# Tail subtraction and state addition moved onto TensorE in the first attention chunks

## The chip, the cores and the metric

The kernel runs on one core of a Trainium2 chip. The metric is device time in microseconds, the median of several executions. The engines are named as the profile names them: PE (TensorE matmuls), PEld (TensorE weight loads), DVE (VectorE), ACT (ScalarE), POOL (GpSimd), and SP, whose queue issues most DMAs.

## The reference, cut to what matters

A linear attention with a decaying state feeds a dense squared-ReLU layer (`_moe_ref`), and that feeds a top-2 mixture of eight experts. Only the attention's recurrence and the first product of the dense layer bear on the change:

```python
for t in range(S):                                    # S = 768, B = 4, H = 8, D = 48
    cur = einsum('bhd,bhe->bhde', u * k[t], v[t])
    y[t] = einsum('bhd,bhde->bhe', r[t], state + cur)
    state = w * state + einsum('bhd,bhe->bhde', k[t], v[t])
x = y as (B*S, H*D)                                   # 3072 x 384
h = x @ w_in;  g = max(h, 0)**2;  x2 = g @ w_out      # then the experts on x2
```

## The kernel before

**Chunks.** The 768 steps of a batch are cut into six chunks of 128, 24 chunks `q` in all; `c = q % 6` is the chunk's place in its batch. A chunk is worked through by steps: `pre` (r*k*u on POOL, and `pre_k`, the scaled keys `kp`), `p_tr` (r and k transposed on PE, copied out as `rT` by DVE and `kT` by ACT), `pre2` (the diagonal: `dg` on DVE, then `am` = ident times `dg` by eight ACT instructions, and `vx`, a small copy of parts of v), `p_a` (the scores r·k on PE into two PSUM banks, laid over `am` by DVE's `copy_predicated`, L468), `p_y` in two parts (y from the state `Z`, then from `am` and v, into one bank), `p_kv` (keys times values on PE, then the new state), and `p_x` (y split for the dense layer).

**State.** In `p_kv`, for `c > 0`, DVE adds the old state to the key-value product (L515, two instructions, one for each half of the partitions), and POOL multiplies the sum by the decay `wmid` (L516, two instructions). For `c == 0` DVE multiplies alone (L518). The last chunk of a batch makes no state.

**Split.** The dense layer's products are made of reduced-precision parts: `p_x` writes `x1h`, the rounded y (ACT, L527), and `x1l`, what rounding left (DVE, L528, y minus `x1h`). `mm1` (L545) multiplies both with the weights' parts; in its very first call the three `x1l` products come last.

**Weights.** While the first chunks run, the 16 pieces of `w_in` and `w_out` are turned from float64 into parts: `conv_w1` on ACT (L273), `conv_w2` on DVE (L280 to L292, four instructions on 128x768 elements), `conv_w3` on ACT (L302) and POOL (L303). A piece lands in one of two buffers `stg`; the end of `conv_w2` frees it and starts the DMA of the next but one.

**Order.** Engines run their instructions in the order of writing. `HEAD` (L27) lists the steps of chunks 0 to 3, with `warm n` = n idle transposes on PE and `load` for DMAs; the tables `CHUNKS` and `CONV_AT` place the steps of later chunks and weights between the dense layer's 16 pairs of `mm1` and `mm2` (L576, L570). PSUM banks of the name `att` are three in rotation, `ph` two: a step that takes a bank waits for the reader of what stood there three (two) banks ago.

Of the kernel before, what the change touches and what calls it, by code (L numbers as in the profile page):

```python
# [8 lines left out]
F32 = mybir.dt.float32  # L9
F32R = mybir.dt.float32r  # L10
BF = mybir.dt.bfloat16
I32 = mybir.dt.int32
AF = mybir.ActivationFunctionType
OP = mybir.AluOpType
# [3 lines left out]
P = 128  # L18
# [5 lines left out]
OWN_ACT = 8  # L24
KP_POOL = (2, 3, 4, 5, 6, 7, 8)

HEAD = ("load_w 0", "p_tr 0 r", "p_tr 0 k", "tables a", "spread", "pre 0",  # L27
# [8 lines left out]

CHUNKS = (((0.72, 2.09, 0.63, 0.83, 1.23, 3.2, 1.96, 5.12, 6.53),
# [56 lines left out]
def body(ctx, tc, r, k, v, w, u, w_in, w_out, w_gate, w_noise, noise, w1, w2, out):  # L94
    nc = tc.nc
    B, H, S, D = r.shape
# [10 lines left out]
    BLK = 512  # L107
    TPB = BLK // P
# [16 lines left out]
    def pool(name, side="left", stack=ctx, **kw):  # L125
        return stack.enter_context(tc.tile_pool(name=name, bufs=1, side=side, reuse_waits="tile", **kw))
# [33 lines left out]
    ident = consts.tile([P, P], F32, name="ident")  # L160
# [11 lines left out]
    def bank(tag="att", bufs=3):  # L172
        return ps.tile([P, 512], F32, name=tag, tag=tag, bufs=bufs)
# [3 lines left out]
    m1 = pool("m1", stack=c_ctx)  # L177
# [30 lines left out]
    def load_next(q):  # L208
        if q < QD or q >= NCH:
            return  # L210
        if q == QD:
            for nm, t in zip("rk", rpt):
                nc.gpsimd.memset(t, 0.0)
                turned[nm] = t.rearrange("p (a x) -> p a x", a=HP)
        load(q, "r")
        b, c = divmod(q, CPB)
        for nm in "rk":
            src = SRC[nm][b, :, c * P:(c + 1) * P, :].rearrange("(a j) s d -> j a (s d)", j=2)
            for j in range(2):
                for o in range(0, D, 32):  # L220
                    nc.sync.dma_start(turned[nm][64 * j + o:64 * j + o + 32, :, :TQ * D - o],
                                      src[j].rearrange("a (s x) -> s a x", x=TQ * D)[:, :, o:])
# [98 lines left out]
    pb = bank()  # L321
# [38 lines left out]
    def warm(n):  # L360
        pw = xops.tile([P, KD, BLK], F32, name="xo")
        for _ in range(n):
            nc.tensor.transpose(pw[:, 0, :P], ident, ident)

    Z = [at.tile([P, HP, 2 * D], F32, name=f"Z{i}") for i in range(2)]
    for t in Z:
        nc.gpsimd.memset(t, 0.0)
# [19 lines left out]
    x1h, x1l = {}, {}  # L387
# [16 lines left out]
    def pairs(q):  # L404
        return L[q]["v"].rearrange("p (a s) d -> p a (s d)", s=2)

    def ends(q):
        t = vx[q % 2].rearrange("p a s x -> p (a s x)")
        return bass.AP(tensor=t.tensor, offset=t.offset, ap=[t.ap[0], [64, HP], [48, 2], [1, 16]])
# [4 lines left out]
    def pre2(q):  # L414
        a, l = A[q], L[q]
        t = a["rk"]
        dg = at.tile([P, H], F32, name="dg", bufs=2)
        nc.vector.tensor_reduce(dg, t, axis=AX.X, op=OP.add)

        own = nc.scalar.copy if q <= TPB else nc.gpsimd.tensor_copy  # L420
        own(ends(q), pairs(q)[:, :, 32:64].rearrange("p a (s x) -> p a s x", s=2))
        a["am"] = at.tile([P, H, P], F32, name="am", tag="am", bufs=2)
        if q < OWN_ACT:
            for h in range(H):
                nc.scalar.activation(a["am"][:, h, :], ident, AF.Copy, scale=dg[:, h:h + 1])
        else:
            nc.gpsimd.tensor_mul(a["am"], ident[:, None, :].to_broadcast([P, H, P]),
                                 dg[:, :, None].to_broadcast([P, H, P]))


    def p_tr(q, which, *tag):
# [41 lines left out]
    def p_y(q, part):  # L473
# [6 lines left out]
        def add(g, x, y, **kw):  # L480
            d, n = divmod(g, 4)
            nc.tensor.matmul(pb[32 * n:32 * n + 32, d, :], x, y, skip_group_check=True, **kw)  # L482

        if part == 0:
            for g in range(KD * 4 if c else 0):
                hp, s = divmod(g, 3)
                add(g, Z[c % 2][:KR, hp, 32 * s:32 * s + 32], a["rT"][:KR, hp, :], start=(g < 4), stop=False)
            return
# [10 lines left out]
    def p_kv(q, *tag):  # L499
        c = q % CPB  # L500
        if c == CPB - 1:
            return
        pb = bank(*tag)[:, :HP * D].rearrange("p (a d) -> p a d", d=D)
        kf = kp[q % 2].rearrange("p h x -> p (h x)")
        v = L[q]["v"]
        for hp in range(HP):
            for g in range(4):
                nc.tensor.matmul(pb[32 * g:32 * g + 32, hp, :], kf[:, hp * P + 32 * g:hp * P + 32 * g + 32],  # L508
                                 v[:, 2 * hp + g // 2, :], start=(hp == 0), stop=(hp == HP - 1), skip_group_check=True)
        for s in range(2):  # L510
            rows = slice(64 * s, 64 * s + D)
            zn = Z[(c + 1) % 2][rows, :, s * D:(s + 1) * D]
            w_ = wmid[rows, :, None].to_broadcast([D, HP, D])
            if c:
                nc.vector.tensor_add(zn, pb[rows], Z[c % 2][rows, :, s * D:(s + 1) * D])  # L515
                nc.gpsimd.tensor_mul(zn, zn, w_)  # L516
            else:
                nc.vector.tensor_mul(zn, pb[rows], w_)  # L518

    def p_x(q, *tag):  # L520
        j, i = divmod(q, TPB)
        if i == 0:
            x1h[j] = m1.tile([P, KD, BLK], F32R, name="x1h", bufs=2)
            x1l[j] = m1.tile([P, KD, BLK], F32R, name="x1l", bufs=2)
        src = A[q]["y"][:, :DM].rearrange("p (d t) -> p d t", t=P)
        hi = x1h[j][:, :, i * P:(i + 1) * P]
        nc.scalar.activation(hi, src, AF.Copy)  # L527
        nc.vector.tensor_tensor(x1l[j][:, :, i * P:(i + 1) * P], src, hi.bitcast(F32), op=OP.subtract)  # L528
        if q + 1 == QD:
            load_next(QD)  # L530
        del A[q], L[q]


    G, PH, XO = {}, {}, {}
    X2 = {}

    def mm1(j, f):
        ph = PH[j, f] = bank("ph", 2)
        qi, fo = divmod(f, NF // NP)
        sl = slice(fo * P, (fo + 1) * P)  # L540
        terms = [(d, wt, xt) for d in range(KD) for wt, xt in ((wih, x1h), (wih, x1l), (wil, x1h))]
        if j == f == 0:
            terms.sort(key=lambda t: t[2] is x1l)
        for n, (d, wt, xt) in enumerate(terms):
            nc.tensor.matmul(ph, wt[qi][:, d, sl], xt[j][:, d, :], start=(n == 0), stop=(n == 3 * KD - 1))  # L545

    def gsplit(j, f):
# [507 lines left out]
    def run(pieces, n):  # L1055
        for p in pieces[:n]:
            p()
        del pieces[:n]

    AW = 3  # L1060
    steps = dict(spread=spread, warm=warm, p_tr=p_tr, pre=pre, tables=tables, pre_k=pre_k, load_w=load_w, p_a=p_a, pre2=pre2, p_kv=p_kv,
                 conv_w1=conv_w1, conv_w2=conv_w2, conv_w3=conv_w3, p_y=p_y, p_x=p_x, load=load)
    for step in HEAD:
        name, *args = step.split()
        tag = ("ph", 2) if name in ("p_kv", "p_x") or "ph" in args else ()
        steps[name](*(int(x) if x.isdigit() else x for x in args if x != "ph"), *tag)

    for j in range(NB):
# [6 lines left out]
        if j + 1 < NB:  # L1075
            for i, at_ in enumerate(CHUNKS[min(j, 2)]):
                q = (j + 1) * TPB + i
                todo = [(pre, ()), (p_tr, "r"), (p_tr, "k"), (pre2, ()), (p_kv, ()), (p_a, ()), (p_y, (0,)), (p_y, (1,)),
                        (p_x, ())]
                for n, (fn, args) in zip(at_, todo):  # L1080
                    if q > TPB or fn not in (pre, p_tr):
                        put(n, fn, q, *args)
# [33 lines left out]
        for f in range(NF):  # L1116
            mm1(j, f)
            gsplit(j, f)
            for p in slots[2 * f]:
                p()  # L1120
            g = j * NF + f - LAG
            if g >= 0:
                mm2(*divmod(g, NF))
                if f == LAG - 1:
                    finish(j - 1)
            for p in slots[2 * f + 1]:
                p()
# [144 lines left out]
```

## Time and profile before

| | us |
|---|---|
| median of 3 runs | 952.46 |
| lowest, highest | 951.77, 954.32 |
| the profiled execution | 953.81 |
| its span in the trace | 952.0 |
| PE busy in the span | 938.3 |
| DVE, ACT, POOL busy | 533.7, 434.4, 345.8 |

The granted TensorE clock is 0.998 of its upper level, 2.4 GHz, over the profiled execution. The span of the trace lies 1.8 us inside the profiled execution's own time; that execution is 1.35 us above the median. In the trace an instruction has a start and a length; a length of a PE row is modelled and overlaps the next, so the pace is read from one start to the next. Waits in brackets give the idle time before a row and what ended it.

### The profile page before, as it was taken

Reading aid. Unit: us, or ns where it says so; the run is one execution under the profiler, and the core shown is the slowest. Engines: PE = TensorE matmul, PEld = TensorE weight load, DVE = VectorE, ACT = ScalarE, POOL = GpSimd, SP = SyncE. Lnnn points to the kernel's source line nnn. Section 1 sums busy time; section 2 is a strip of 40 time slices with the busy share of each in tenths; the row PEclk is TensorE's granted clock in tenths of the full one; section 3 lists DMA queues with packets and bytes.
Section 4 is the critical chain, followed back from the end, with each engine's and each line's share of the span. In section 5 each row is a group of like instructions: output and inputs, shape, how many; then the busy total and the mean of one; then the engine's idle time right before and its main releaser. Section 6 shows DMA issues by size and latency. Waiting matters only on the chain.

```text
span 952.0 us, 17757 instructions
## 1 busy us (share of the span) xinstructions
PE 938.3 (99%) x6845; PEld 805.0 (85%) x6845; DVE 533.7 (56%) x985; ACT 434.4 (46%) x798; POOL 345.8 (36%) x401
## 2 busy tenths in 40 slices
PE   9899999999999999999999999999999999999997
PEld 7677787778778778877888899999999898989987
DVE  8999757535835663583254564554545555456420
ACT  6766655334434434353555542443444444444321
POOL 6665353544563372545030353122121221212112
PEclk9999999999999999999999999999999999999999
DMA  8655379932444272342024357466645565645212
GB/s 182 161 163 164 99 192 301 245 108 64 118 121 106 55 189 57 106 108 77 1 101 98 103 137 183 108 135 135 130 97 114 121 117 109 117 94 111 33 21 37
DMA packets 193233, 112.32 MB, mean 118 GB/s; under 512 B 131777, under 2 KB 185698, under 8 KB 193122
## 3 DMA queue, kind: packets, MB, share of 16 engines
q1 hardware_dynamic: 181698, 91.03, 37.5%
q0 software_dynamic: 10624, 19.74, 11.2%
q8 instruction: 75, 1.23, 0.5%
q14 instruction: 36, 0.29, 0.1%
q10 hardware_dynamic: 800, 0.02, 0.0%
HBM read 74.64 MB, written 36.12 MB: 116 GB/s over the span
## 4 chain that ended last, share of the span: by engine, by line
PE 90%; DVE 5%; DMA 1%; issue 1%; ACT 1%; POOL 0%; POOLq 0%; ACTq 0%; DVEq 0%; SPq 0%
PE ph L545 20%; PE xo L576 19%; PE ph L866 19%; PE y L923 14%; PE y L954 4%; PE att L482 3%; PE ph L954 2%; PE att L464 2%; PE att L609 2%; PE y L866 2%; PE xo L570 1%; PE att L967 1%; DVE t L281 1%; PE att L508 1%; DVE am L468 1%
## 5 line engine op out<-in xcount | busy, mean ns | idle before, releaser
L934 POOL DMA_INDIRECT out<-yt,id x56 | 87.2, 1556 | 297.8 <-ACT yt L932 257.2
L560 DVE TENSOR_TENSOR gl<-g,gh 128x512 fp32r<-128x512 f32 x90 | 76.2, 846 | 134.9 <-ACT gh L558 131.4
L909 DVE SCALAR_TENSOR_TENSOR hl<-ph,hh 128x512 fp32r<-128x512 f32 (+1 forms) x112 | 66.9, 599 | 113.4 <-ACT hh L908 109.4
L550 ACT ACTIVATE rt<-ph 128x512 f32<-128x512 f32 x96 | 57.2, 596 | 157.9 <-PE ph L545 138.9
L545 PE MATMUL ph<-x1h,wih 128*128 128x512 f32 x288 | 119.3, 414 | 0.0
L866 PE MATMUL ph<-xh,w0h 128*128 128x512 f32 (+3 forms) x336 | 118.1, 352 | 0.0
L866 PE MATMUL ph<-xl,w0h 128*128 128x512 f32 (+3 forms) x336 | 116.2, 346 | 0.2 <-DVE xl L835 0.2
L866 PE MATMUL ph<-xh,w0l 128*128 128x512 f32 (+3 forms) x336 | 116.2, 346 | 0.0
L545 PE MATMUL ph<-x1h,wil 128*128 128x512 f32 x288 | 112.5, 391 | 0.0
L545 PE MATMUL ph<-x1l,wih 128*128 128x512 f32 x288 | 112.3, 391 | 0.0
L576 PE MATMUL xo<-gh,wol 128*128 128x512 f32 x270 | 106.2, 394 | 0.0
L908 ACT ACTIVATE hh<-ph 128x512 fp32r<-128x512 f32 (+1 forms) x112 | 58.7, 525 | 89.0 <-PE ph L866 82.1
L923 PE MATMUL y<-w1h,hh 128*128 128x384 f32 x256 | 85.7, 335 | 0.0
L923 PE MATMUL y<-w1l,hh 128*128 128x384 f32 x256 | 85.6, 334 | 0.0
L923 PE MATMUL y<-w1h,hl 128*128 128x384 f32 x256 | 85.6, 334 | 0.0
L737 POOL DMA_INDIRECT sent<-row,si x48 | 50.6, 1055 | 63.9 <-DVE gl L560 45.0
L576 PE MATMUL xo<-gh,woh 128*128 128x512 f32 x180 | 71.6, 398 | 0.0
L576 PE MATMUL xo<-gl,woh 128*128 128x512 f32 x180 | 70.2, 390 | 0.0
L866 PEld LDWEIGHTS ph<-xl,w0h 128*128 128x128 f32 x336 | 63.3, 189 | 7.7 <-DVE xl L835 0.9
L866 PEld LDWEIGHTS ph<-xh,w0l 128*128 128x128 f32 x336 | 63.2, 188 | 7.7
L866 PEld LDWEIGHTS ph<-xh,w0h 128*128 128x128 f32 x336 | 63.3, 188 | 7.0 <-ACT xh L834 0.3
L545 PEld LDWEIGHTS ph<-x1h,wih 128*128 128x128 f32 x288 | 54.0, 188 | 16.5 <-issue 3.3
(235 smaller groups left out, 2138.7 us busy)
## 6 DMA issues: line engine op xcount, KB each, us to landing
ws<-in_moe_w SPq DMA_DIRECT2D x128, 96.0 KB
ws<-in_moe_w SPq DMA_DIRECT2D x32, 384.0 KB
sent<-zero SPq DMA_DIRECT2D x8, 1375.5 KB
G<-sent SPq DMA_DIRECT2D x36, 192.0 KB
stg<-in_moe_w_in SPq DMA_DIRECT2D x8, 768.0 KB
stg<-in_moe_w_out SPq DMA_DIRECT2D x8, 768.0 KB
out<-zero SPq DMA_DIRECT2D x5, 960.0 KB
lv<-in_v SPq DMA_DIRECT2D x24, 192.0 KB
```

What stands on the lines that cost most here:

```text
L482: nc.tensor.matmul(pb[32 * n:32 * n + 32, d, :], x, y, skip_group_check=True, **kw)
L545: nc.tensor.matmul(ph, wt[qi][:, d, sl], xt[j][:, d, :], start=(n == 0), stop=(n == 3 * KD - 1))
L550: nc.scalar.activation(rt, ph, AF.Relu)
L560: nc.vector.tensor_tensor(gl, g, gh.bitcast(F32), op=OP.subtract)
L576: nc.tensor.matmul(XO[j][:, d, :], wt[qi][:, fo, sl], gt, start=(f == 0 and n == 0), stop=(f == NF - 1 and n == 2))
L737: st = nc.gpsimd.indirect_dma_start(out=sent, in_=s["row"][:, i, :], in_offset=None, out_offset=bass.IndirectOffsetOnAxis(ap=s["si"][:, i, ...
L866: nc.tensor.matmul(ph[:, c], wt[:, d, sl], xt[:, d, c], start=(m == 0), stop=(m == 3 * KD - 1))
L908: nc.scalar.activation(hh[:, :n], ph, AF.Relu)
L909: nc.vector.scalar_tensor_tensor(hl[:, :n], ph, 0.0, hh[:, :n].bitcast(F32), op0=OP.max, op1=OP.subtract)
L923: nc.tensor.matmul(py, ht[:, sl], wt[:, fo, :], start=(m == 0), stop=(m == 3 * NF2 - 1))
L934: st = nc.gpsimd.indirect_dma_start(out=out, in_=yt, in_offset=None, compute_op=OP.add, out_offset=bass.IndirectOffsetOnAxis(ap=IDX[e, un] ...
L954: nc.tensor.matmul(py[d][:, c], wt[:, fo, sl], ht[:, c], start=(m == 0), stop=(m == 3 * NF2 - 1))
```

## The change

In chunks 1 to 4 (`q <= TPB`, the second to the fifth of batch 0) PE adds the old state to the key-value product in PSUM, with two multiplications by the identity (48 rows and 192 columns each, float32, on the two halves of the partitions, into one bank); DVE then multiplies by the decay out of PSUM, and POOL's two instructions are gone. For chunks 0 to 3 the new step `p_rest` makes `x1l`: PE adds `x1h` times minus the identity (128x384) onto y's bank, and ACT copies out what remains. `p_rest 0` to `p_rest 2` stand in `HEAD`, `p_rest 3` inside the first `mm1`, behind its third product. `minus` is made by one ACT instruction ahead. In `HEAD` the ACT part of `pre2 2` now stands behind `p_rest 0`, and in all chunks `vx` is written behind `am` instead of ahead of it.

```diff
@@ pre2
-        own = nc.scalar.copy if q <= TPB else nc.gpsimd.tensor_copy
-        own(ends(q), pairs(q)[:, :, 32:64].rearrange("p a (s x) -> p a s x", s=2))
         a["am"] = at.tile([P, H, P], F32, name="am", tag="am", bufs=2)
...
+        own = nc.scalar.copy if q <= TPB else nc.gpsimd.tensor_copy
+        own(ends(q), pairs(q)[:, :, 32:64].rearrange("p a (s x) -> p a s x", s=2))
@@ p_kv
-            if c:
+            if c and q <= TPB:
+                nc.tensor.matmul(pb[rows], ident[rows, rows], Z[c % 2][rows, :, s * D:(s + 1) * D],
+                                 start=False, stop=True, skip_group_check=True)
+                nc.vector.tensor_mul(zn, pb[rows], w_)
+            elif c:
                 nc.vector.tensor_add(zn, pb[rows], Z[c % 2][rows, :, s * D:(s + 1) * D])
                 nc.gpsimd.tensor_mul(zn, zn, w_)
@@ p_x
-        nc.vector.tensor_tensor(x1l[j][:, :, i * P:(i + 1) * P], src, hi.bitcast(F32), op=OP.subtract)
+        lo = x1l[j][:, :, i * P:(i + 1) * P]
+        if q < TPB:
+            REST[q] = src, hi, lo
+        else:
+            nc.vector.tensor_tensor(lo, src, hi.bitcast(F32), op=OP.subtract)
@@ new
+    minus = m1.tile([P, BLK], F32R, name="minus", tag="rt", bufs=1)[:, :P]
+    nc.scalar.activation(minus, ident, AF.Copy, scale=-1.0)
+    def p_rest(q):
+        src, hi, lo = REST.pop(q)
+        nc.tensor.matmul(src, minus, hi, start=False, stop=True, skip_group_check=True)
+        nc.scalar.activation(lo, src, AF.Copy)
@@ mm1
+            if j == f == 0 and n == 3:
+                p_rest(TPB - 1)
@@ HEAD
-        "p_tr 2 k ph", "pre 3", "pre2 2", "warm 10", "p_a 1"
+        "p_tr 2 k ph", "pre 3", "warm 10", "p_rest 0", "pre2 2", "p_a 1"
...
-        "p_tr 3 k ph", "pre2 3", "p_a 2"
+        "p_tr 3 k ph", "p_rest 1", "pre2 3", "p_a 2"
...
-        "p_y 3 0", "p_kv 3"
+        "p_y 3 0", "p_rest 2", "p_kv 3"
```

PE between the transposes of chunk 2 and the state part of y of chunk 1 (`rp`, `kp` feed the transposes, `lv,kp` the key-value product of chunk 1, `rT,kT` its scores), before:

```order
L444 MATMUL att<-ident,rp_95 112x128 x4
L508 MATMUL ph<-lv,kp_98 32x48 x16
L444 MATMUL ph<-ident,kp_97 112x128 x4
L363 MATMUL xo<-ident 128x128 x10
L464 MATMUL att<-rT,kT 128x128 x8
L482 MATMUL att<-rT,Z_206 32x128 x12
```

And now:

```order
L448 MATMUL att<-ident,rp_95 112x128 x4
L512 MATMUL ph<-lv,kp_98 32x48 x16
L519 MATMUL ph<-Z_208,ident 48x192 x2
L448 MATMUL ph<-ident,kp_97 112x128 x4
L364 MATMUL xo<-ident 128x128 x10
L548 MATMUL att<-x1h,minus 128x384
L468 MATMUL att<-rT,kT 128x128 x8
L486 MATMUL att<-rT,Z_208 32x128 x12
```

The state's pair (L519) stands ahead of the transposes of k, and the subtraction (L548) ahead of the scores; the same two stand in the same places of chunk 2.

DVE from the scores of chunk 2 to the split of chunk 3, before:

```order
L468 COPY_PREDICATED am<-mask,att 128x4x128 x2
L280 TENSOR_SCALAR t_524<-t_524 128x768
L281 TENSOR_SCALAR t_524<-t_524 128x768
L282 SCALAR_TENSOR_TENSOR t_524<-stg,t_524 128x768
L468 COPY_PREDICATED am<-mask,ph 128x4x128 x2
L528 TENSOR_TENSOR x1l<-att,x1h 128x3x128
L292 SCALAR_TENSOR_TENSOR t_524<-stg,t_524 128x768
L449 TENSOR_TENSOR rT<-att,pow 112x512
L515 TENSOR_TENSOR Z_205<-ph,Z_206 48x4x48 x2
L528 TENSOR_TENSOR x1l<-att,x1h 128x3x128
```

And now:

```order
L472 COPY_PREDICATED am<-mask,att 128x4x128 x2
L281 TENSOR_SCALAR t_526<-t_526 128x768
L282 TENSOR_SCALAR t_526<-t_526 128x768
L283 SCALAR_TENSOR_TENSOR t_526<-stg,t_526 128x768
L472 COPY_PREDICATED am<-mask,ph 128x4x128 x2
L293 SCALAR_TENSOR_TENSOR t_526<-stg,t_526 128x768
L453 TENSOR_TENSOR rT<-att,pow 112x512
L521 TENSOR_TENSOR Z_207<-ph,wmid 48x4x48 x2
```

Two `x1l` are gone from this piece (two more stood ahead of it), and the state's add has become a multiplication of the same size.

ACT from y of chunk 2 to the dense layer's first ReLU (`rt`), before:

```order
L527 ACTIVATE x1h<-att 128x3x128
L273 ACTIVATE t_624<-stg 128x768
L527 ACTIVATE x1h<-att 128x3x128
L302 ACTIVATE wih_125<-t_524 128x768
L453 ACTIVATE kT<-att 112x512
L550 ACTIVATE rt<-ph 128x512
```

And now:

```order
L535 ACTIVATE x1h<-att 128x3x128
L274 ACTIVATE t_627<-stg 128x768
L549 ACTIVATE x1l<-att 128x3x128
L535 ACTIVATE x1h<-att 128x3x128
L303 ACTIVATE wih_125<-t_526 128x768
L457 ACTIVATE kT<-att 112x512
L549 ACTIVATE x1l<-att 128x3x128
L569 ACTIVATE rt<-ph 128x512
```

The last `x1l` of the block stands behind a weight piece and a transposed k on ACT, where DVE had made it.

## Rows read from the trace of the kernel before

**Rows 1.** Busy time by stretch: stretch, length, PE, PEld, DVE, ACT, POOL, granted clock, DMA.

```profile
12.00:42.00 30.00, 27.14 (x495) 21.50 (x495) 29.06 (x43) 20.97 (x54) 19.97 (x20) 1.00 0.75 184
42.00:73.00 31.00, 30.22 (x207) 21.68 (x207) 28.90 (x32) 20.76 (x39) 18.64 (x13) 1.00 0.54 160
73.00:400.00 327.00, 325.97 (x2602) 257.90 (x2602) 198.60 (x378) 154.30 (x274) 155.99 (x166) 1.00 0.51 138
```

**Rows 2.** The chain that ended last, in order of time: start, length, what.

```profile
23.74 0.56 DVE x1l L528
...
40.15 0.26 DVE Z L515
...
56.34 4.80 DMA stg<-in_moe_w_in
...
62.13 4.28 DMA stg<-in_moe_w_out
...
71.85 1.07 PE att L482 x28
```

**Rows 3.** Waits of PE from 8 to 80 us: total, times, longest.

```profile
PE att L482 <- DVE am L468: 0.8, 3, 0.4
```

**Rows 4.** PE in order of time: start, length, line, out<-in [idle before <-releaser].

```profile
6.95 0.91 PE L356 MATMUL att<-us 1*128 1x384 f32 x2
7.79 0.66 PE L351 MATMUL att<-ident,back 128*128 128x128 f32 x4
...
17.77 1.74 PE L464 MATMUL att<-rT,kT 48*128 48x128 f32 x16
19.59 0.86 PE L482 MATMUL att<-rT,Z 112*32 112x128 f32 x24
...
23.33 1.16 PE L464 MATMUL att<-rT,kT 48*128 48x128 f32 x16
24.43 1.20 PE L363 MATMUL xo<-ident 128*128 128x128 f32 x9
...
30.65 0.55 PE L508 MATMUL ph<-lv,kp 128*32 128x48 f32 x32 [0.89 <-DVE am L468]
...
38.71 0.49 PE L464 MATMUL att<-rT,kT 48*128 48x128 f32 x2
40.95 1.13 PE L464 MATMUL att<-rT,kT 48*128 48x128 f32 x14 [1.75 <-DVE Z L515]
```

**Rows 5.** PE near the end: products of 128x384, one behind the other.

```profile
942.32 0.33 PE L923 MATMUL y<-w1l,hh 128*128 128x384 f32 x1
942.50 0.33 PE L923 MATMUL y<-w1h,hh 128*128 128x384 f32 x1
```

**Rows 6.** DVE in order of time: state, a weight piece beside POOL, one without.

```profile
24.67 1.35 DVE L468 COPY_PREDICATED am<-mask,att 128x512 f32<-128x512 uint16 x2
...
33.81 0.56 DVE L528 TENSOR_TENSOR x1l<-att,x1h 128x384 fp32r<-128x384 f32 x1
34.28 0.68 DVE L280 TENSOR_SCALAR t<-t 128x768 f32<-128x768 f32 x1
...
40.83 1.46 DVE L280 TENSOR_SCALAR t<-t 128x768 f32<-128x768 f32 x1
...
53.14 0.55 DVE L280 TENSOR_SCALAR t<-t 128x768 f32<-128x768 f32 x1
```

**Rows 7.** ACT in order of time, around the split of chunks 0 to 3.

```profile
22.56 0.49 ACT L527 ACTIVATE x1h<-att 128x384 fp32r<-128x384 f32 x1
...
32.78 0.84 ACT L302 ACTIVATE wih<-t 128x768 fp32r<-128x768 f32 x1
33.52 0.59 ACT L453 ACTIVATE kT<-att 112x512 f32<-112x512 f32 x1
```

**Rows 8.** POOL's last state multiplication before 45 us, and who waited for L516.

```profile
41.83 1.61 POOL L516 TENSOR_TENSOR Z<-Z,wmid 48x192 f32<-48x192 f32 x2
...
  PEld att L464: 0.2, 1
```

More of the change, by code (lines that the diff above doesn't have):

```diff
@@ L25 @@
 KP_POOL = (2, 3, 4, 5, 6, 7, 8)
-HEAD = ("load_w 0", "p_tr 0 r", "p_tr 0 k", "tables a", "spread", "pre 0",
[8 rows of a table removed]
+HEAD = ("load_w 0", "p_tr 0 r", "p_tr 0 k", "tables a", "spread", "pre 0", "tables b",
[9 rows of a table added]
 CHUNKS = (((0.72, 2.09, 0.63, 0.83, 1.23, 3.2, 1.96, 5.12, 6.53),
@@ L363, in warm @@
             nc.tensor.transpose(pw[:, 0, :P], ident, ident)
+    REST = {}
+    minus = m1.tile([P, BLK], F32R, name="minus", tag="rt", bufs=1)[:, :P]
+    nc.scalar.activation(minus, ident, AF.Copy, scale=-1.0)
     Z = [at.tile([P, HP, 2 * D], F32, name=f"Z{i}") for i in range(2)]
@@ L1060, in body @@
     AW = 3
-    steps = dict(spread=spread, warm=warm, p_tr=p_tr, pre=pre, tables=tables, pre_k=pre_k, load_w=load_w, p_a=p_a, pre2=pre2, p_kv=p_kv,
+    steps = dict(p_rest=p_rest, spread=spread, warm=warm, p_tr=p_tr, pre=pre, tables=tables, pre_k=pre_k, load_w=load_w, p_a=p_a, pre2=pre2, p_kv=p_kv,
                  conv_w1=conv_w1, conv_w2=conv_w2, conv_w3=conv_w3, p_y=p_y, p_x=p_x, load=load)
```

17 rows, old and new, of the table HEAD are left out of this document.

## The prediction

> **What bounds the kernel now.** I read three views. First the busy times by stretch: from 73 us to 400 us PE is busy 325.97 of 327 us [rows 1], so whatever reaches 73 us earlier keeps its gain for hundreds of us; nothing that I see later in the trace takes it back. Between 12 and 42 us PE is busy 27.14 of 30 us, but DVE 29.06 [rows 1]: here the two hand the work to and fro, and the change lies in this stretch. Then the chain of waits: from 23.74 us on it runs through DVE (x1l at 23.74, the state's add at 40.15), then twice through a DMA of weights that a finished conversion sets off (4.80 and 4.28 us), and it passes to PE for good only at 71.85 [rows 2]. Last PE itself in order of time, for the places where it stands. It waits 0.89 us for a bank ahead of the key-value product of chunk 3 and 1.75 us ahead of the scores of chunk 4, the latter for the state's add on DVE [rows 4]; in the second part of y it waits 0.8 us in three pieces [rows 3]. One loss is no wait in the list: the scores of chunk 1 take 1.82 us (17.77 to 19.59) where those of chunk 2 take 1.10 (23.33 to 24.43) [rows 4], 0.72 lost. Together 0.9 + 1.8 + 0.8 + 0.7 = 4.2 us: no more than that can be won here, and PE gets new work that has to come out of it.
>
> **The change part by part.**
>
> *The subtraction on PE.* Four products of 128x384. Such products follow each other at 942.32 and 942.50 [rows 5], so 0.18 us each, 0.7 us in all.
>
> *The state on PE.* Four pairs of 192 columns in float32 on 48 rows, one on each half of the partitions. No such pair is in the trace. From below: the scores also run as pairs on the two halves, 8 products of 128 columns in 1.10 us [rows 4], 0.275 a pair, times 192/128 = 0.41 us. From above: one float32 product of 384 columns, so the same columns one behind the other, fills 0.84 us up to the next start (6.95 to 7.79) [rows 4]. That it costs nothing is excluded: PE has no gap at its place. I take 0.41, since the scores have the same 48 rows and halves, and keep 0.84.
>
> Here a page speaks against the change. In the scores the two halves write two banks, in the new pair one. The Trainium skill, TensorEngine Tiling (Array Packing), section Gotcha 1: PSUM Pressure, says that different row tiles cannot access the same PSUM bank simultaneously. By it the pair would run one after the other, near the upper end; by the row of the scores, near the lower. No row of this trace has two halves in one bank.
>
> *What DVE loses.* Four x1l. One takes the stretch from 33.81 to 34.28 [rows 6], 0.47 us, 1.9 us in all. The state's multiplication out of PSUM replaces an add of the same size: no difference.
>
> *What POOL loses.* Four state multiplications; the one at 41.83 took 1.61 us [rows 8]. PE was held up by this line for 0.2 us in the whole kernel [rows 8], so their going gains nothing directly. But DVE's weight instruction L280 took 1.46 us at 40.83, just ahead of that row, and 0.55 at 53.14 [rows 6]: some of DVE's instructions are longer when POOL works. With the state gone, POOL leaves DVE alone there earlier. I put 0.3 us on it, between 0 and the 0.9 that these two rows differ by.
>
> *What ACT gets.* Four x1l copies and one for `minus`. A split of the same size takes 0.49 us (22.56) [rows 7], 2.0 us in all; ACT is busy 20.97 of 30 us [rows 1]. `minus` is made ahead of the first y and has no one waiting. What stands behind the copies: the diagonal `am` of chunk 2, `am` of chunk 3, and at the end the first ReLU. `vx` behind `am` costs nothing: both are needed by the same step on PE, and `am` has to pass through DVE first. POOL's `vx` of later chunks likewise; its cover is that PE waits for nothing after 73 us [rows 1]; without it, it would cost the length of one `am`.
>
> *Walk through the block.* (1) Chunk 1: the pair and `p_rest 0` add 0.41 + 0.18 = 0.59 ahead of the scores of chunk 1. These lost 0.72 waiting for `rT`; so the end of the scores stays where it was, about 19.6. The cover is just used up. (2) Chunk 2: the pair and `p_rest 1` add 0.59 ahead of the scores at 23.33 [rows 4], with no wait there to pay for it: they start at 23.9 and end at 25.0. DVE's `copy_predicated` that reads them started at 24.67 [rows 6]; now it can't before 25.1. DVE is 0.45 us late, although it has shed two x1l: it waits for PE in their place. This is where half of the saving goes. (3) From there DVE is the bound up to 40 us, as the chain has it. It sheds the x1l of chunk 2 (0.47): even with before. PE's wait ahead of the key-value product of chunk 3 (30.65) stays, shifted by 0.4. (4) It sheds the x1l of chunk 3 (0.47): the state's add of chunk 4, at 40.15 [rows 2], is due 0.5 us earlier. (5) PE has by then got all of its new work: two more pairs and two more subtractions, 1.2 us, of which about 1.0 is visible, so it reaches the scores of chunk 4 at 38.71 + 1.0 = 39.7 and waits there until 40.95 - 0.5 = 40.45 [rows 4]: a wait of 0.75 instead of 1.75, end 0.5 us earlier. (6) On the way to 71.85 the chain is DVE, then the two DMAs, ACT, DVE [rows 2]. All of it starts with the end of a conversion, so it moves as a whole by 0.5 and by the 0.3 that POOL leaves. PE follows, because its waits of 0.8 [rows 3] are for this chain.
>
> Sum: -0.5 - 0.3 = **-0.8 us**. Against the profiled execution this is 952.0 - 0.8 = 951.2 in the span; that execution lies 1.35 us above the median, so the median should be 952.46 - 0.8 = **951.7**.
>
> **The rivals.**
>
> *A. As forecast*, 951.7, by itself 951.0 to 952.4.
>
> *B. The pair runs one after the other* (0.84), and the change is even. Each pair costs 0.43 more. Two of them stand ahead of the scores of chunk 2, so step (2) is 0.86 later, and DVE's 0.5 in step (4) turns into -0.4; PE reaches chunk 4 about when before it went on. The 0.3 of POOL is left: 952.46 + 0.4 - 0.3 = 952.5. The change then doesn't do what it is there for: DVE's free time is spent waiting for PE. For it: no gap on PE between 19.59 and 24.43 that would hide the pair, and the one bank. The page named above would give this time.
>
> *C. DVE keeps all that it sheds.* 1.9 us and the whole 0.9 of POOL would be 952.46 - 2.8 = 949.7; but steps (1) and (2) hang on scores that PE can't bring before 19.6 and 24.5 even if its new work were free, so that of the first two x1l at most 0.2 counts: 0.2 + 0.94 + 0.6 = 1.7, so 950.7, with 949.8 as the end. It needs pairs well under 0.41.
>
> *D. ACT is late with the last x1l, and the kernel is slower.* The x1l of chunk 3 now stands behind a weight piece (0.84 at 32.78, which itself waits for DVE's conversion) and `kT` (0.59 at 33.52) [rows 7], and the first dense product waits for it; the ReLU, and with it DVE's work up to the state of chunk 4, stands behind. I find x1l ready at about 35.2 and PE there at 35.1, so almost even. Each us of lateness delays PE by a us; the wait of 0.75 in step (5) and the 0.8 gained have to be used up first. It decides against the change from about 1.6 us of lateness; at 2.5 us it is +0.9, 953.4. Against it: ACT has 9 idle us in this stretch [rows 1].
>
> **How the numbers follow.** Chances: A 0.45, B 0.25, C 0.18, D 0.12. About 0.3% (2.9 us) is what a measurement of this kernel can tell from no change: faster means under 949.6, slower over 955.3. A and B lie inside by far. Of C some 0.06 lies under 949.6 (the ceiling of 4.2 allows it), of D some 0.05 over 955.3, and another 0.02 and 0.01 I give to what I have not seen. So faster 0.08, same 0.86, slower 0.06. The range goes from the end of C to D: 949.8 to 953.6, with about 0.08 left out below and 0.1 above.
>
> **What would show it.** In the profile after: the pair's length from one start to the next (0.41 or 0.84) and the subtraction's (0.18); the scores of chunk 1 ending at 19.6 again; DVE's `copy_predicated` for chunk 2 at about 25.1 with an idle time ahead of it that ends with PE; PE's wait ahead of the scores of chunk 4 cut to about 0.75 us, and their rest starting at 40.4; the first weights piece's DMA that stood at 56.34 at 55.5; the chain passing to PE at about 71.0. If DVE is not idle ahead of 25.1, step (2) is wrong. If the three x1l products in the first dense product start over 0.5 us after the sixth, D is at work. If all of this holds and the time still differs by over 1 us, something after 73 us has moved that I hold to be fixed.

## The result, and the profile after

The changed kernel takes 961.59 us (median of 4 runs, 961.49 to 962.41); the kernel before, on the same chip, 952.96 us (4 runs, 951.77 to 954.32). The ratio is 1.009, with 1.0078 to 1.0102 as its 95% interval: 8.6 us slower, where 951.7 us was forecast and 953.6 us was the end of the range. The span grew from 952.0 to 959.9 us.

Busy time by stretch after the change, with the columns of [rows 1]:

```profile
12.00:42.00 30.00, 25.34 (x454) 19.46 (x451) 22.16 (x34) 17.93 (x49) 12.62 (x11) 0.94 0.65 153
42.00:73.00 31.00, 28.49 (x212) 20.37 (x212) 24.32 (x31) 20.14 (x39) 12.46 (x8) 0.94 0.46 136
73.00:400.00 327.00, 327.00 (x2650) 258.15 (x2649) 208.95 (x379) 156.66 (x280) 162.42 (x169) 1.00 0.52 141
```

Beside [rows 1], all engines are busy for less time in the first two stretches, PE by 1.8 and 1.7 us, DVE by 6.9 and 4.6 us. No engine has become the bound; they wait for each other. And the granted clock, 1.00 before, is 0.94 in both. From 73 us on PE has no gap left, where it had 1.03 us before. So the loss lies ahead of 73 us, as the change does.

Whom PE waits for, in the whole span (total, times, longest), the lines with the change's product:

```profile
PE ph L519 <- DVE Z L521: 4.3, 3, 2.6
PE att L519 <- DVE Z L521: 2.5, 1, 2.5
```

L519 is the new product that adds the state, L521 is DVE's multiplication by the decay that stands behind it in the code. PE waits 6.8 us for the instruction that is meant to wait for PE. None of the waits of [rows 3] and [rows 4] is left in the list.

PE in order of time after the change (start, length, line, tiles, count, and the idle time ahead with what ended it):

```profile
16.77 0.52 PE L519 MATMUL ph<-Z,ident 48*48 48x192 f32 x2
19.86 0.52 PE L519 MATMUL ph<-Z,ident 48*48 48x192 f32 x2 [2.57 <-DVE Z L521]
20.31 0.65 PE L448 MATMUL ph<-ident,kp 128*112 128x128 f32 x4
20.80 1.82 PE L364 MATMUL xo<-ident 128*128 128x128 f32 x10
22.26 0.67 PE L548 MATMUL att<-x1h,minus 128*128 128x384 f32 x1
22.86 2.05 PE L468 MATMUL att<-rT,kT 48*128 48x128 f32 x16
24.84 0.86 PE L486 MATMUL att<-rT,Z 112*32 112x128 f32 x24
...
28.96 0.52 PE L519 MATMUL ph<-Z,ident 48*48 48x192 f32 x2 [0.44 <-DVE Z L521]
...
39.35 0.52 PE L519 MATMUL ph<-Z,ident 48*48 48x192 f32 x2 [1.32 <-DVE Z L521]
...
47.62 0.52 PE L519 MATMUL att<-Z,ident 48*48 48x192 f32 x2 [2.51 <-DVE Z L521]
...
81.06 0.86 PE L486 MATMUL att<-rT,Z 112*32 112x128 f32 x24
```

The two halves of a state, which the prediction counted as one block, stand 3.1 us apart in chunk 1: the first runs at 16.77, the second at 19.86. Each half is itself 0.45 us long (19.86 to 20.31). DVE's rows tell why:

```profile
17.19 1.64 DVE L283 SCALAR_TENSOR_TENSOR t<-stg,t 128x768 int32<-128x768 int32 x1
18.86 0.69 DVE L453 TENSOR_TENSOR rT<-att,pow 112x512 f32<-112x512 f32 x1
19.47 0.34 DVE L521 TENSOR_TENSOR Z<-ph,wmid 48x192 f32<-48x192 f32 x1
20.42 0.36 DVE L521 TENSOR_TENSOR Z<-ph,wmid 48x192 f32<-48x192 f32 x1 [0.61 <-PE ph L519]
...
42.49 2.51 DVE L293 SCALAR_TENSOR_TENSOR t<-stg,t 128x768 int32<-128x768 int32 x1
46.03 0.69 DVE L579 TENSOR_TENSOR gl<-g,gh 128x512 fp32r<-128x512 f32 x1 [1.04 <-ACT gh L577]
...
47.22 0.35 DVE L521 TENSOR_TENSOR Z<-att,wmid 48x192 f32<-48x192 f32 x1
```

The loop in `p_kv` writes product (half 0), multiplication (half 0), product (half 1), multiplication (half 1), and all four use one tile in PSUM. The second product writes a tile that the first multiplication reads, so it waits for that multiplication, although the two touch different partitions. The multiplication in turn stands in DVE's queue behind a weight conversion (1.64 us) and `rT`. In chunk 4 it stands behind a conversion of 2.51 us and the dense layer's `gl`, which itself waits for ACT. Then the roles turn round, and in chunk 1 DVE waits 0.61 us for the second product.

Fine stretches of the same kernel (columns as above) show the second price:

```profile
20.00:22.00 2.00, 2.00 (x15) 1.71 (x15) 0.91 (x2) 0.60 (x1) 0.76 (x1) 0.83 1.07 189
22.00:24.00 2.00, 2.00 (x14) 1.67 (x14) 0.00 (x0) 1.03 (x4) 0.00 (x0) 0.50 0.06 13
...
37.00:42.00 5.00, 3.61 (x74) 2.41 (x75) 4.28 (x8) 1.54 (x3) 0.00 (x0) 1.00 0.51 151
...
48.00:52.00 4.00, 4.00 (x32) 2.98 (x32) 3.40 (x5) 2.05 (x8) 0.65 (x1) 0.58 0.15 59
```

Behind the waits of 2.57 and 2.51 us the granted clock falls to 0.50, the lower level of 1.2 GHz; behind the wait of 1.32 us (37 to 42 us) it doesn't. So the scores of chunk 1, at 22.86, take 2.05 us, where the same sixteen rows at full clock take 1.16 (the scores of chunk 2, at 23.33 in [rows 4]).

Where the block ends: the last state part of y ahead of 100 us starts at 81.06 us (the last row of PE above). In the kernel before it started at 70.36:

```profile
70.36 0.86 PE L482 MATMUL att<-rT,Z 112*32 112x128 f32 x24
```

That is 10.7 us later, of which some 8 us are left at the end. This start, in us, serves as a mark in the experiments; it is read from the one profiled execution of each kernel.

### The profile page after: what moved, and what is told of

It reads as the page before. It is cut to its first block, busy times and chain, and to the rows that moved or that the text cites. A ratio compares the mean times of both kernels' runs of the same rounds, so it can differ in the third digit from the quotient of the medians.

```text
span 959.9 us, 17783 instructions
## 1 busy us (share of the span) xinstructions
PE 943.9 (98%) x6865; PEld 808.9 (84%) x6865; DVE 536.6 (56%) x981; ACT 437.1 (46%) x803; POOL 340.9 (36%) x393
## 4 chain that ended last, share of the span: by engine, by line
PE 95%; DVE 2%; ACT 1%; issue 1%; POOL 0%; POOLq 0%; DVEq 0%; ACTq 0%
PE ph L564 22%; PE xo L595 20%; PE ph L885 19%; PE y L942 13%; PE y L973 4%; PE att L486 4%; PE att L468 3%; PE ph L973 2%; PE att L628 2%; PE y L885 2%; PE xo L589 2%; PE att L986 1%; PE att L512 1%; PE att L448 1%; PE att L324 0%
## 5 line engine op out<-in xcount | busy, mean ns | idle before, releaser
L579 DVE TENSOR_TENSOR gl<-g,gh 128x512 fp32r<-128x512 f32 x90 | 82.3, 915 | 147.9 <-ACT gh L577 147.8
```

Source lines behind the costliest of these rows:

```text
L579: nc.vector.tensor_tensor(gl, g, gh.bitcast(F32), op=OP.subtract)
```

## The experiments

Medians of different sessions differ (the kernel before gave 952.96, 954.28 and 955.13 us), so the table gives ratios to the kernel before of the same session.

| kernel | us | ratio to before (95%) | mark |
|---|---|---|---|
| before | | 1 | 70.36 |
| after | 961.59 | 1.0090 (1.0078 to 1.0102) | 81.06 |
| state_only | 964.72 | 1.0104 (1.0086 to 1.0122) | 82.30 |
| filled | 961.33 | 1.0069 (1.0054 to 1.0085) | 77.97 |
| pair_first | 955.16 | 1.0009 (0.9999 to 1.0018) | 71.04 |
| state_pair_first | 955.19 | 1.0001 (0.9991 to 1.0010) | 71.62 |
| rest_only | 953.20 | 0.9990 (0.9981 to 0.9999) | 69.75 |
| vx_only | 955.87 | 1.0005 (0.9996 to 1.0014) | 71.59 |
| chunk1_as_before | 955.68 | 1.0005 (0.9994 to 1.0016) | 70.32 |
| rest_state4 | 954.68 | 0.9992 (0.9982 to 1.0001) | 70.55 |

### pair_first: both products ahead of both multiplications

On the changed kernel, nothing but the order of writing inside `p_kv`:

```diff
+        if c and q <= TPB:
+            for s in range(2):
+                rows = slice(64 * s, 64 * s + D)
+                nc.tensor.matmul(pb[rows], ident[rows, rows], Z[c % 2][rows, :, s * D:(s + 1) * D], ...)
         for s in range(2):
...
             if c and q <= TPB:
-                nc.tensor.matmul(pb[rows], ident[rows, rows], ...)
                 nc.vector.tensor_mul(zn, pb[rows], w_)
```

> The changed kernel with one edit: both halves of the state are added on TensorE before VectorE multiplies the first half, so that no product of TensorE stands behind a multiplication. Theory 1 (the 6.8 us that TensorE waits in the profile of the changed kernel ahead of the second halves, and the lower granted clock behind two of these waits, are the whole loss): the waits ahead of the state's products go to nearly 0, the granted clock is 1.00 throughout, and the time is 952.2 us, 0.8 below the kernel before, within 951.0 to 953.5. Theory 2 (the subtraction on TensorE and ScalarE is what costs, the split of the pair little): 958 us or more. Price of the pair: 0.4 to 0.5 us from the first start to the next work if the halves overlap, 0.9 if not.

Measured: 1.0009 instead of 1.0090, so 7.7 us come back with the order of four instructions. All work is still there. PE in order of time:

```profile
15.95 0.53 PE L517 MATMUL ph<-Z,ident 48*48 48x192 f32 x4
16.41 0.65 PE L448 MATMUL ph<-ident,kp 128*112 128x128 f32 x4
...
18.10 0.44 PE L551 MATMUL att<-x1h,minus 128*128 128x384 f32 x1
18.47 0.48 PE L468 MATMUL att<-rT,kT 48*128 48x128 f32 x2
19.65 1.16 PE L468 MATMUL att<-rT,kT 48*128 48x128 f32 x14 [0.70 <-DVE rT L453]
20.74 0.86 PE L486 MATMUL att<-rT,Z 112*32 112x128 f32 x24
```

Both halves together now take 0.46 us (15.95 to 16.41), as long as one alone did. The clock holds 0.999 over the span. The wait of the second product is thus shown to be the cause, and the pair itself to be about what was forecast. What is left is a kernel that is even with the one before, not 0.8 us faster; PE still waits 0.70 us ahead of the scores of chunk 1, for `rT`.

### state_only: the state part alone, in the change's order

On the kernel before, only the change to `p_kv` (products and multiplications in turn).

```diff
-            if c:
+            if c and q <= TPB:
+                nc.tensor.matmul(pb[rows], ident[rows, rows], Z[c % 2][rows, :, s * D:(s + 1) * D], ...)
+                nc.vector.tensor_mul(zn, pb[rows], w_)
+            elif c:
                 nc.vector.tensor_add(zn, pb[rows], Z[c % 2][rows, :, s * D:(s + 1) * D])
```

> The state on TensorE alone, written as the change writes it (product, multiplication, product, multiplication); the subtraction stays on VectorE and everything else as before. Theory 1: the loss is here, 959 to 963 us, with waits of 5 us or more ahead of the second halves. Theory 2: 953 to 955 us.

Measured: 1.0104. The whole loss comes with this part (the interval holds the change's 1.0090). Whom PE waits for:

```profile
PE ph L515 <- DVE Z L517: 4.9, 3, 2.7
PE att L515 <- DVE Z L517: 2.4, 1, 2.4
```

It is 7.3 us, against 6.8 in the full change, where DVE has less to do. Here the wait of chunk 3 is 1.79 us instead of 1.32, and the clock falls behind it too (last but two of the columns):

```profile
38.62 0.52 PE L515 MATMUL ph<-Z,ident 48*48 48x192 f32 x2 [1.79 <-DVE Z L517]
```

```profile
40.00:42.00 2.00, 2.00 (x15) 1.72 (x8) 1.21 (x3) 1.71 (x3) 0.47 (x1) 0.51 1.06 362
```

Of its four executions the one with a mean clock of 0.996 took 962.21 us, the three with 0.990 and 0.991 took 964.11 to 965.72.

### rest_only: the subtraction alone

On the changed kernel, with the state as before and `vx` ahead of `am` again (these lines are left out here).

```diff
...
-            if c and q <= TPB:
+            if False:
```

> The subtraction on TensorE alone, with the places that the change gives it; the state is added by VectorE and multiplied by GpSimd as before, and v's small copy stands ahead of the diagonal as before. Theory 1: no loss, 951.5 to 953 us (four products of 0.18 us added, four VectorE subtractions taken away). Theory 2: 957 us or more.

Measured: 0.9990 (0.9981 to 0.9999), about 1 us less, with an interval that just leaves out no change. PE's wait ahead of the scores of chunk 4, 1.75 us in [rows 4], and DVE ahead of chunk 2:

```profile
40.43 1.13 PE L468 MATMUL att<-rT,kT 48*128 48x128 f32 x14 [0.56 <-DVE Z L523]
```

```profile
24.95 1.37 DVE L472 COPY_PREDICATED am<-mask,att 128x512 f32<-128x512 uint16 x2 [0.56 <-PE att L468]
```

This is what steps (2) and (5) of the prediction described: DVE stands idle ahead of its `copy_predicated` until PE has the scores, and the scores of chunk 4 go on at 40.43 after a wait cut to 0.56. The steps fit the subtraction without the state. That the 24.95 lies near the forecast of 25.1 is in part luck: the forecast had a pair of 0.41 us and a subtraction of 0.18 ahead of the scores, and this kernel has no pair there and a subtraction of 0.37 (23.32 to 23.69).

Part of the 1 us may be the clock. All 11 executions of rest_only had a mean clock of 0.998 or 0.999; of the 21 of the kernel before in the same session, 18 had 0.994 to 0.997, and the three with 0.998 had a median of 953.81 us, 0.6 above rest_only. The runs don't separate the shorter wait from the clock that it may have kept up.

### filled: the wait kept, PE's idle time filled

The changed kernel, with 20, 4, 10 and 20 idle transposes on PE between the halves in chunks 1 to 4. They take the place of waiting; the second product still comes after DVE.

```diff
             if c and q <= TPB:
+                if s:
+                    warm((0, 20, 4, 10, 20)[q])
                 nc.tensor.matmul(pb[rows], ...
```

> The changed kernel with idle transposes between the two halves of the state (20 for chunk 1, 4, 10 and 20 for chunks 2 to 4), in the time in which TensorE waits anyway. Theory 1: the waits of 2.6, 1.3 and 2.5 us are filled and nothing is won from them, but TensorE has no idle stretch, so the granted clock stays at its upper level and the slow stretches behind the waits (half clock over some 5 us in all, about 3 us of time) are gone: 958.5 us, 3 below the changed kernel. If the clock is not part of the loss: 961.5 or more, since the transposes only add work.

Measured: 1.0069, so 0.21% less than the change, 2.0 us. PE in order of time, then the busy time of the first stretch (columns as above):

```profile
16.74 2.40 PE L364 MATMUL xo<-ident 128*128 128x128 f32 x20
19.87 0.52 PE L521 MATMUL ph<-Z,ident 48*48 48x192 f32 x2 [0.73 <-DVE Z L523]
...
22.17 1.16 PE L468 MATMUL att<-rT,kT 48*128 48x128 f32 x16
```

```profile
12.00:42.00 30.00, 28.95 (x462) 22.52 (x463) 23.66 (x35) 18.72 (x49) 13.68 (x12) 1.00 0.69 166
```

The second half runs at the same time as in the change (19.87 against 19.86), but the clock stays at 1.00 and the scores take 1.16 us. From 42 to 73 us it is 1.00 as well. So the clock is worth about 2 us of the loss by the medians (3 were expected, and the two intervals just overlap) and 3.1 by the mark. What pair_first gives back beyond this (1.0069 against 1.0009, 5.7 us) is put down to the waiting and the split halves.

### state_pair_first: the state part alone, pairs together

On the kernel before, the products of both halves first, as in pair_first.

```diff
+        if c and q <= TPB:
+            for s in range(2):
...
+                nc.tensor.matmul(pb[rows], ident[rows, rows], Z[c % 2][rows, :, s * D:(s + 1) * D], ...)
...
-            if c:
+            if c and q <= TPB:
+                nc.vector.tensor_mul(zn, pb[rows], w_)
+            elif c:
```

> The kernel before with the state on TensorE alone, both halves added before VectorE multiplies; the subtraction on VectorE and v's small copy as before. The version with the pair ahead and everything else of the change stood 0.9 us above the kernel before, the subtraction alone 1.1 below. Theory 1 (the two parts are worth what they are worth apart, the state about +2 us: four pairs of 0.46 on TensorE, and GpSimd's work for chunk 3 that now runs into VectorE's conversion of the first weights): 1.5 to 2.5 us above the kernel before. Theory 2 (the state is free by itself and the two parts get in each other's way): within 0.7 us of the kernel before.

Measured: 1.0001 (0.9991 to 1.0010): the loss that was expected didn't come. In its one profile PE waits 1.34 us for `rT` ahead of the scores of chunk 1 and the mark is 1.3 us late, and the median shows nothing of that. The mark of one execution doesn't foretell the median to better than about 1 us here.

### vx_only: vx behind am, alone

On the kernel before, the two lines of `own` moved behind `am`, as in the change.

```diff
-        own = nc.scalar.copy if q <= TPB else nc.gpsimd.tensor_copy
-        own(ends(q), pairs(q)[:, :, 32:64].rearrange("p a (s x) -> p a s x", s=2))
         a["am"] = at.tile([P, H, P], F32, name="am", tag="am", bufs=2)
...
+        own = nc.scalar.copy if q <= TPB else nc.gpsimd.tensor_copy
+        own(ends(q), pairs(q)[:, :, 32:64].rearrange("p a (s x) -> p a s x", s=2))
```

> The kernel before with v's small copy behind the diagonal in all chunks, nothing else. Theory 1: no difference, within 0.5 us of the kernel before, both in the first chunks (ScalarE) and in the later ones (GpSimd). Rival: the copy ahead of the first conversion on ScalarE delays VectorE's first weights by 0.2 to 0.3 us and that shows.

Measured: 1.0005 (0.9996 to 1.0014), no difference that can be told. Its profile has one thing of use: PE's wait before the scores of chunk 4 is the same 1.75 us as in [rows 4], but the clock behind it fell here:

```profile
41.67 1.81 PE L464 MATMUL att<-rT,kT 48*128 48x128 f32 x14 [1.75 <-DVE Z L515]
```

```profile
42.00:44.00 2.00, 2.00 (x15) 1.69 (x12) 1.93 (x3) 2.00 (x9) 1.93 (x3) 0.50 0.81 323
```

In the kernel before the 14 products took 1.13 us [rows 4].

### chunk1_as_before: pair_first, with chunk 1's state as before

This asks what remains in pair_first: in it PE waits for `rT` of chunk 1, which stands on DVE behind conversions that run beside POOL. DVE and POOL of pair_first, in order of time:

```profile
14.68 1.24 DVE L281 TENSOR_SCALAR t<-t 128x768 f32<-128x768 f32 x1 [0.23 <-ACT t L274]
15.96 1.24 DVE L282 TENSOR_SCALAR t<-t 128x768 int32<-128x768 int32 x1
17.23 1.64 DVE L283 SCALAR_TENSOR_TENSOR t<-stg,t 128x768 int32<-128x768 int32 x1
18.91 0.69 DVE L453 TENSOR_TENSOR rT<-att,pow 112x512 f32<-112x512 f32 x1
```

```profile
16.75 1.32 POOL L416 TENSOR_TENSOR kp<-lk,tk 128x384 f32<-128x384 f32 x1
```

In both places, that of the products and that of the multiplication:

```diff
-        if c and q <= TPB:
+        if 2 <= q <= TPB:
```

> The version with the pair ahead, but for chunk 1 the state is added by VectorE and multiplied by GpSimd as before (chunks 2 to 4 on TensorE). GpSimd then waits again for VectorE before it scales the keys of chunk 3. Theory 1 (collision): VectorE's third conversion instruction, 1.64 us in the version with the pair ahead and 0.96 in the kernel before, is back at 0.96, its copy of r for chunk 2 starts at about 17.9 in place of 18.9, TensorE's wait of 0.70 for it in the scores of chunk 1 shrinks to 0.3 or less, and the time is 1 us below the version with the pair ahead, even with the kernel before. Theory 2 (only TensorE's work counts): one pair less, 0.5 us below at most, and the conversion stays long.

Measured: 1.0005 (0.9994 to 1.0016). DVE, and POOL's state:

```profile
17.11 0.96 DVE L283 SCALAR_TENSOR_TENSOR t<-stg,t 128x768 int32<-128x768 int32 x1
18.10 0.69 DVE L453 TENSOR_TENSOR rT<-att,pow 112x512 f32<-112x512 f32 x1
```

```profile
19.13 1.08 POOL L527 TENSOR_TENSOR Z<-Z,wmid 48x192 f32<-48x192 f32 x2 [2.47 <-DVE Z L526]
```

With POOL tied to the state again, it sits idle for 2.47 us, DVE's third conversion instruction takes 0.96 us instead of 1.64, and `rT` is 0.8 us earlier. The collision is shown; its price in the median is below what these runs resolve (1.0005 against 1.0009).

### rest_state4: the subtraction, and the state of chunk 4 alone

On rest_only, with the state on PE for chunk 4 only, pairs together.

```diff
+        if q == TPB:
+            for s in range(2):
...
+                nc.tensor.matmul(pb[rows], ident[rows, rows], Z[c % 2][rows, :, s * D:(s + 1) * D],
...
-            if False:
...
+            if q == TPB:
                 nc.vector.tensor_mul(zn, pb[rows], w_)
```

> The subtraction alone, with the state on TensorE only for chunk 4 (pair ahead). Theory 1: GpSimd's last state multiplication, which ran beside VectorE's conversion at 41 us, is gone, TensorE gets one pair of 0.46 us in front of scores that waited 0.56 us in the version with the subtraction alone: 0 to 0.5 us below that version, so 1.1 to 1.6 us below the kernel before, the best of all. Theory 2: TensorE bound, 0.5 us above that version.

Measured: 0.9992 (0.9982 to 1.0001). The wait ahead of the scores of chunk 4 is gone, but PE now waits 0.8 us for ACT's `x1h` ahead of a subtraction, and the 0 to 0.5 us below rest_only that were expected didn't come.

No version beats the kernel before by more than about 0.1%.

## Why the prediction was wrong

**The step that failed** is "*The state on PE* ... I take 0.41", used in step (1) as "the pair and `p_rest 0` add 0.41 + 0.18 = 0.59". It priced four pairs as work of PE and put no wait on them. On PE the two products do follow each other with nothing between, and the order of PE's instructions counts them in one line (L519 x2). But an engine's own order doesn't tell what the other engine does between. The diff did: in the loop over `s`, DVE's multiplication of half 0 stands between the products, on the same tile. With it, the step would have read: in each of four chunks PE waits until DVE comes to that multiplication, and DVE's rows in order of time would have told when that is.

By the rows of after, the step costs 2.57 + 0.44 + 1.32 + 2.51 = 6.84 us of waiting, four halves that no longer overlap (4 x 0.45 = 1.8 us) and about 2 us of clock: 10.6 us. Between after and pair_first the mark moves by 81.06 - 71.04 = 10.0. At the end 7.7 us of it are left.

**"Whatever reaches 73 us earlier keeps its gain for hundreds of us"** holds only roughly, and for a loss too: the mark is 10.7 us late, the end of the span 7.9 (959.9 against 952.0). From the mark to the next dense product PE takes 1.67 us after the change (81.06 to 82.73) where it took 2.48 (70.36 to 72.84), with one of the waits for `am` of [rows 3] in it; that gives back 0.8. About another 1 us lies at the one gap that the kernel before has between 73 and 400 us, which is no wait for another engine in the profile:

```profile
200.61 0.42 PE L482 MATMUL att<-rT,Z 112*32 112x128 f32 x5 [1.03 <-issue]
```

After the change PE has no gap there; why, no run shows. In pair_first it went the other way, by another 0.8 us between 71 and 112 us: a piece of weights issued at 76.08 reached ACT only at 81.77, where the kernel before needed from 75.55 to 79.89, and DVE stood idle 2.57 us for it. Whether that transfer is longer because of the edit or in that one execution is open: in chunk1_as_before the same piece, issued at 75.34, about when it was before, took 6.7 us.

**The pair itself** was right in size: 0.46 us together, near the 0.41 of the scores' rows. A second product on the other half of the partitions adds next to nothing even in one bank (0.46 for both, 0.45 for one). So rival B, which needed 0.84 us, was not at work. The rule of the Trainium skill, TensorEngine Tiling (Array Packing), section Gotcha 1: PSUM Pressure, that different row tiles cannot access the same PSUM bank simultaneously, isn't borne out by these rows, in which the two halves write different partitions of the bank.

**The subtraction** was sized at 0.18 us from a row of equals. Inside the first `mm1` it is 0.18 (42.30 to 42.48 after the change), but ahead of the scores 0.37 (18.10 to 18.47 in pair_first). As a part it does about what was forecast for the whole: rest_only gains about 1 us, but by other terms than the forecast's.

**POOL's relief** of 0.3 us did not show, and in chunk 1 the rows go the other way. The row of 1.46 us at 40.83, from which the prediction sized it, ran for the most part beside another instruction of POOL than the state's, which starts at 41.83:

```profile
40.04 1.83 POOL L303 TENSOR_TENSOR wol<-t,woh 128x768 fp32r<-128x768 f32 x1 [3.36 <-ACT woh L302]
```

Freed from the state, POOL doesn't leave DVE alone. In pair_first it starts `kp` of chunk 3 at 16.75 us instead of 19.79, beside DVE's third conversion instruction, which then takes 1.64 us where it took 0.96 in the kernel before. (The second took 1.24 there too; the first, 1.24 against 0.68, runs beside `ra` at 14.50.) The prediction asked what POOL's instructions held up, not what POOL would do in the time won. The Trainium skill, SBUF — State Buffer, section Who interferes with whom, names VectorE and GpSimd as the two engines that block each other at a shared pair of ports, and says that the order of issue decides which of them is held up. That DVE's same instruction took 0.96 us beside an idle POOL and 1.64 beside a busy one agrees with the first; the second isn't settled here, since `kp` too took 1.32 us instead of 1.01.

**The walk.** Step (1), scores of chunk 1 ending at 19.6 again, is wrong in after (24.84) and in pair_first (20.74). Step (2), DVE idle until PE brings the scores of chunk 2, is right in kind in pair_first (0.59 us, at 26.38) and close in rest_only (24.95, forecast not before 25.1). Step (5), the wait of 1.75 us cut, holds in rest_only (0.56 at 40.43) and goes further in pair_first, where no wait is left there. Step (6), the chain moving as a whole, holds up to the first DMA in rest_only too: the DMA of [rows 2] at 56.34 starts at 55.69 there, forecast 55.5.

**The other rivals.** C didn't come, since nothing like its gain appeared. D, ACT late with the last `x1l`, was not at work: in after the `x1l` products of `mm1` start right behind the others, at 43.23 (PE in order of time, with the subtraction of chunk 3 ahead).

```profile
42.30 0.34 PE L548 MATMUL att<-x1h,minus 128*128 128x384 f32 x1
42.48 0.40 PE L564 MATMUL ph<-x1h,wil 128*128 128x512 f32 x1
...
42.95 0.39 PE L564 MATMUL ph<-x1h,wil 128*128 128x512 f32 x1
43.23 0.96 PE L564 MATMUL ph<-x1l,wih 128*128 128x512 f32 x3
```

What happened lay outside all four. The chances (slower 0.06) rested on [rows 3] and [rows 4], where PE had only 4.2 us to win and little that could be lost; the loss came from a wait that no row of before could show, but that the order of the code did. Of the 0.06, 0.05 were given to D and 0.01 to what had not been seen, and what came was of the latter.

**What stays open.** With the order mended, the change gives +0.9 us (-0.1 to +1.7) where -0.8 was forecast. The subtraction alone gives -1.0, the state in pairs +0.1, `vx` +0.5, the last two within their noise. The three add up to -0.4, 1.3 us less than the whole, with about 0.9 us of uncertainty on each. Whether the parts harm each other (the collision of POOL and DVE, the piece of weights at 76 us) or this is noise, the runs don't tell.

## What to carry to other kernels

When two engines share a tile in a loop over its parts, write all of the one engine's work first and all of the other's after it: product, read, product, read on one tile makes the first engine wait for the second engine's queue, however short the work is, and here the order of four instructions was worth 7.7 us. Before pricing an added instruction, look in the code for what the other engines do on the same tile between it and its neighbours; a list of one engine's own instructions doesn't show that. And when work is taken off an engine, ask what it will run instead and beside whom.

## What was unexpected of the hardware

- The granted clock fell from 2.4 to 1.2 GHz behind PE's waits of 2.57 and 2.51 us, and not behind those of 0.44 and 1.32. Behind a wait of 1.75 us it fell in the profile of vx_only and not in that of the kernel before, and behind one of 1.79 it fell in state_only. Ten transposes took 1.46 us from start to start (20.80 to 22.26), the subtraction 0.60 (22.26 to 22.86) and the scores 1.98 (22.86 to 24.84). Where idle transposes filled the waits it stayed at 1.00, and the time was 2.0 us lower by the ratios, whose intervals just overlap.
- Two float32 products of 48 rows by 192 columns, on two halves of the partitions and into one bank, take 0.46 us together and 0.45 each when apart.
- The same product of 128x384 took 0.18 us from start to start in the first `mm1` and 0.37 between idle transposes and scores.
- DVE's conversion (128x768, int32) took 0.96 us beside an idle POOL and 1.64 us beside a busy one, at the same place of the program.
